# An mLSTM recurrence moved one chunk further ahead of the FFN that consumes it

## The chip, the cores and the metric

The kernel runs on one core of one Trainium2 chip. The metric is the device time of one execution in microseconds; the time of a kernel is the median of its runs. A profile is one further execution, recorded instruction by instruction.

TensorE multiplies matrices and accumulates in PSUM. VectorE and ScalarE work on tiles in SBUF and PSUM, GpSimd on tiles in SBUF. SyncE only issues DMAs, one after the other in the order of the program: where one waits, all behind it wait too. In profile rows the engines are PE (matmul), PEld (weight load), DVE (VectorE), ACT (ScalarE), POOL (GpSimd) and SPq (SyncE's queue).

## What is computed

An mLSTM cell (4 batches, 8 heads, 768 steps, head dimension 40) whose output, as 3072 tokens of 320 numbers, goes through a feed-forward network with squared ReLU. The reference, cut:

```python
for t in range(S):
    m_new = np.maximum(f_gate[:, :, t] + m, i_gate[:, :, t])
    f_stab = np.exp(f_gate[:, :, t] + m - m_new)
    i_stab = np.exp(i_gate[:, :, t] - m_new)
    m = m_new
    C = f_stab[:, :, None, None] * C + i_stab[:, :, None, None] * np.einsum('bhd,bhe->bhde', vt, kt)
    n = f_stab[:, :, None] * n + i_stab[:, :, None] * kt
    h_tilde = np.einsum('bhde,bhe->bhd', C, qt)
    nq = np.einsum('bhd,bhd->bh', n, qt)[:, :, None]
    denom = np.maximum(np.abs(nq), 1.0)
    o = 1.0 / (1.0 + np.exp(-o_gate[:, :, t]))
    y[:, :, t] = o * h_tilde / denom
# x: y as (3072, 320); w_in is 320 x 2048, w_out 2048 x 320
h = np.maximum(x @ w_in, 0.0)
out = h * h @ w_out
```

## The kernel before

**Tiling.** The sequence is cut into chunks of 128 steps: 6 chunks in each of 4 batches, 24 chunks in all, numbered 0 to 23. Within a chunk the recurrence is done as attention: scores k·q (`scores`, L423), times a matrix W of decays (`weighted`, L436, into the tiles `P_sb`), times v, plus the state C carried from the chunk before. At the first chunk of a batch there is no old state, at the last no new one. Two chunks form a group of the FFN, 12 groups. FFN1 (x by w_in, L644 and L655) has four parts per group, FFN2 (squares by w_out) four as well; from group 1 on FFN2 is done with seven half-size products instead of eight (`ffn2_fast`, L738), for which VectorE makes sums and differences of the squares (`sums`, L733).

**The path of a chunk's x in the second stage** (chunks 6 to 23), where transposes are made by VectorE in 32x32 squares and by DMAs that move the squares. `attend_turned` (L522, L511, L533) leaves numerators in PSUM; VectorE transposes them into `tn` (L544, one buffer); `store_num` (L556) writes them to DRAM, `load_num` (L561, four DMAs) reads them back in other order; `normalise_turned` (L573 to L582) divides and multiplies by the output gate into x; `store_rows` (L608) and `load_rows` (L613, four DMAs) take x through DRAM; `turn_squares` (L620) transposes the squares in place, and only then can FFN1 read x. Keys and queries take a like path: `pair_up` (L287, four DMAs within DRAM), `load_squares` (L309, four), `turn_kq` (L316). The decays come from `load_A` (L334, one DMA of 512 KB), exponentials on ScalarE (`decays` L369, `weigh` L383) and a mask on GpSimd (L359).

**The order** is written out by hand; every engine runs its instructions in the order in which the code issues them. A first stage (the loop over `u`, lines 873 to 930) does chunks 2 to 5 with FFN1 of groups 0 and 1, while the weights are fetched and rounded. The second stage is the loop over `parts` (line 977): entries (1, g, i) are parts of FFN1 of group g, (2, g, i) of FFN2. Entries 0 to 7 are FFN1 of group 2 and FFN2 of group 0. From entry 8 on a period has eight entries, `r` = 0 to 7: two parts of FFN2 of group g (r = 0, 1), four of FFN1 of group g+2 (r = 2 to 5), the other two of FFN2 (r = 6, 7). The parts of FFN1 go in pairs: two times L644, two times L655, and then `tiled()`, here called the tiled section: one chunk is attended and the scores of the next are made. So a period has two tiled sections, in r = 3 and r = 5. In the kernel before they attend chunks `a` = 6 + 2(n // 8) and a+1, while FFN1 reads chunks a−2 and a−1.

Buffers that matter: two `P_sb` tiles, so the tiles of the next chunk are those of the one before; four banks for scores and numerators; two `A_bc`, two `kqT`, two `xT` (one per group).

## Time and profile before

| | |
|---|---|
| runs | 7: 557.88 to 561.87 us, median 559.99 |
| profiled execution | 562.97 us, span of the profile 561.2 us |
| mean granted TensorE clock | 0.973 |
| busy share of the span | PE 94%, VectorE 59%, ScalarE 34%, GpSimd 16% |
| DMA | 68.06 MB, 56.5% of 16 engines' span in SyncE's queue |

A timeline row gives the start in us from the span's start, the time to the end of the last of its instructions, engine, line, operation, tiles, shape and count; in brackets the idle time ahead of the first one, and what ended it. A row of a window gives the window, its length, each engine's busy time with the number of instructions, and then TensorE's granted clock, the DMA share and GB/s. A row of DMAs gives how many, KB each, and the median time from issue to landing in us. One matmul of the program is recorded as two.

### The profile page before, as it was taken

To read this page: it belongs to the slowest core of one execution; us is meant where nothing else is said; L and a number is where in the kernel's file an instruction comes from. 1 tells how busy PE (TensorE), PEld (TensorE's weight loads), DVE (VectorE), ACT (ScalarE), POOL (GpSimd) and SP (SyncE) were. 2 spreads that over 40 slices of the span, in tenths; PEclk is the share of its full clock that TensorE was granted. 3 is DMA by queue.
4 is the path that set the end of the run, shared out by engine and by line. 5 is a ranking of instruction groups with operands and counts; after the bars stand their busy time and mean duration, and the time that the engine had idled before them with its cause. 6 is when DMAs were issued, how large, how long until landed. Compare 5 with 4: busy or idle time off the path is not lost.

```text
span 561.2 us, 10358 instructions
## 1 busy us (share of the span) xinstructions
PE 525.7 (94%) x3932; PEld 454.9 (81%) x3933; DVE 333.6 (59%) x638; ACT 192.6 (34%) x460; POOL 88.4 (16%) x110
## 2 busy tenths in 40 slices
PE   9998999999999699969979969988997999999997
PEld 4877887876988588958968958887896898898997
DVE  8579988678745437536645553753763764561351
ACT  3766587442361215304114331321532312101100
POOL 3336633132020001001001000110200100000000
PEclk9998999999999989979989998998999999999999
DMA  9979899766646827645764572782774460220000
GB/s 196 226 163 202 161 206 220 168 141 152 118 100 151 166 25 179 131 86 109 161 122 84 140 152 40 172 168 42 179 146 72 119 122 10 76 71 1 25 23 25
DMA packets 239394, 68.06 MB, mean 121 GB/s; under 512 B 185744, under 2 KB 233872, under 8 KB 239344
## 3 DMA queue, kind: packets, MB, share of 16 engines
q1 hardware_dynamic: 239248, 67.20, 56.5%
q8 instruction: 31, 0.51, 0.4%
q10 hardware_dynamic: 96, 0.20, 0.1%
q14 instruction: 19, 0.16, 0.1%
HBM read 55.08 MB, written 17.86 MB: 130 GB/s over the span
## 4 chain that ended last, share of the span: by engine, by line
PE 49%; DMA 22%; SPq 15%; DVE 8%; issue 3%; ACT 2%; POOL 0%; DVEq 0%; POOLq 0%
PE h_ps L644 25%; DMA x_rows<-x_sb 8%; PE h_ps L738 8%; PE h_ps L655 6%; SPq L613 5%; DMA xT<-x_rows 4%; DMA kq<-num_rows 3%; SPq L561 3%; DMA num_rows<-tn 3%; SPq L287 2%; DMA A_bc<-a_rows 2%; SPq L309 2%; PE tp L423 2%; PE numT L533 1%; PE idle L797 1%
## 5 line engine op out<-in xcount | busy, mean ns | idle before, releaser
L644 PE MATMUL h_ps<-xT,w_in 128*128 128x256 f32 x768 | 185.5, 402 | 27.9 <-DVE xT L620 18.1
L644 PEld LDWEIGHTS h_ps<-xT,w_in 128*128 128x128 f32 x768 | 152.3, 202 | 54.7 <-DVE xT L620 29.4
L670 ACT ACTIVATE r_sb<-h_ps 128x512 f32<-128x512 f32 x96 | 49.8, 599 | 163.1 <-issue 95.1
L677 DVE TENSOR_TENSOR g<-r_sb 128x512 f32<-128x512 f32 x96 | 69.7, 774 | 11.6 <-ACT r_sb L670 11.6
L738 PE MATMUL h_ps<-w_out,g 128*128 128x160 f32 x528 | 75.7, 299 | 0.0
L738 PEld LDWEIGHTS h_ps<-w_out,g 128*128 128x128 f32 x528 | 72.9, 190 | 0.4 <-DVE y_sb L754 0.2
L544 DVE STREAM_TRANSPOSE tn<-numT 128x256 f32<-128x256 f32 x36 | 15.8, 447 | 85.1 <-PE numT L533 84.6
L383 ACT ACTIVATE W_sb<-A_bc,b_T 128x128 f32<-128x128 f32 x176 | 53.8, 388 | 30.6 <-POOL A_bc L359 30.4
L738 PE MATMUL h_ps<-T,S 128*128 128x160 f32 x352 | 52.3, 302 | 0.0
L738 PEld LDWEIGHTS h_ps<-T,S 128*128 128x128 f32 x352 | 48.7, 190 | 1.4 <-ACT r_sb L670 0.3
L655 PE MATMUL h_ps<-xT,w_in 64*128 64x256 f32 x384 | 49.0, 391 | 0.0
L655 PEld LDWEIGHTS h_ps<-xT,w_in 64*128 64x128 f32 x384 | 34.8, 186 | 12.3 <-issue 9.3
L359 POOL TENSOR_SCALAR_AFFINE_SELECT A_bc<-A_bc 128x1024 f32<-128x1024 f32 x22 | 25.4, 1156 | 107.5 <-ACT kq L369 107.5
L754 DVE TENSOR_TENSOR y_sb<-y_sb,h_ps 128x160 f32<-128x160 f32 x44 | 13.7, 312 | 37.5 <-PE h_ps L738 37.5
L758 ACT COPY y_sb<-h_ps 128x160 f32<-128x160 f32 x11 | 3.2, 292 | 93.6 <-PE h_ps L738 93.6
L436 DVE TENSOR_TENSOR P_sb<-tp,W_sb 128x512 f32<-128x512 f32 x46 | 29.6, 686 | 8.3 <-PE tp L423 6.1
L620 DVE STREAM_TRANSPOSE xT<-xT 128x384 f32<-128x384 f32 x18 | 10.3, 573 | 40.6 <-DMA xT<-x_rows 40.6
L489 POOL TENSOR_TENSOR Cd<-C,kq 128x164 f32<-128x164 f32 x15 | 7.0, 464 | 165.3 <-DVE C L550 131.9
L423 PE MATMUL tp<-kqT 40*128 40x128 f32 x384 | 27.7, 284 | 1.1 <-ACT xT L629 1.1
L423 PEld LDWEIGHTS tp<-kqT 40*128 40x128 f32 x384 | 23.5, 187 | 5.2 <-issue 3.2
L395 POOL TENSOR_TENSOR vw<-va,W_sb 128x328 f32<-128x328 f32 x20 | 17.4, 872 | 54.0 <-ACT W_sb L383 37.0
L738 PE MATMUL h_ps<-w_out,S 128*128 128x160 f32 x176 | 25.7, 299 | 0.0
(119 smaller groups left out, 613.2 us busy)
## 6 DMA issues: line engine op xcount, KB each, us to landing
A_bc<-a_rows SPq DMA_DIRECT2D x23, 512.0 KB, 5.2
raw<-in_moe_w_out_dram SPq DMA_DIRECT2D x16, 320.0 KB, 3.5
num_rows<-tn SPq DMA_DIRECT2D x18, 256.0 KB, 2.4
kq<-num_rows SPq DMA_DIRECT2D x72, 64.0 KB, 2.1
kqT<-kq_rows SPq DMA_DIRECT2D x34, 128.0 KB, 3.2
raw<-in_moe_w_in_dram SPq DMA_DIRECT2D x8, 512.0 KB, 4.3
kq<-in_k_dram SPq DMA_DIRECT2D x24, 160.0 KB, 3.7
va<-in_v_dram SPq DMA_DIRECT2D x24, 160.0 KB, 4.1
```

The lines of the kernel that those rows point to most:

```text
L359: nc.gpsimd.affine_select(A[:], A[:], compare_op=ALU.is_ge, fill=-1e30, base=0, pattern=[[0, H], [1, P]], channel_multiplier=-1,)
L383: nc.scalar.activation(d["W"][:, i * n + h, :], A[i][:, h, :], AF.Exp, bias=b_T[:, b, c, i * n + h : i * n + h + 1],)
L395: nc.gpsimd.tensor_tensor(d["vw"][:], d["va"][:], d["W"][:, :, P - 1 : P].to_broadcast([P, H, D1]), op=ALU.mult,)
L423: nc.tensor.matmul(sc[i][:, j, :], lhsT=d["kT"][rows, j, :], rhs=d["qT"][rows, j, :], start=True, stop=True,)
L436: nc.vector.tensor_tensor(t, d["sc"][i], d["W"][:, heads, :], op=ALU.mult)
L561: nc.sync.dma_start(N[m * SQ : (m + 1) * SQ].rearrange("p (e c) -> p e c", c=P), n_d[s, :, m * P : (m + 1) * P].rearrange("(e p) c -> p e ...
L613: nc.sync.dma_start(t[r * SQ : (r + 1) * SQ].rearrange("p (b a) -> p b a", a=SQ), x_d[s, :, :, r * SQ : (r + 1) * SQ].rearrange("c (n p) a ...
L644: nc.tensor.matmul(hs[i][:, n, :], lhsT=w_in[:, a, fb * P : (fb + 1) * P], rhs=xT[:, :, a, :], start=(n == 0 and a == 0), stop=False,)
L655: nc.tensor.matmul(hs[i][:, n, :], lhsT=w_in2[rows, 2 * pp + n, :], rhs=xT[rows, :, 2, :], start=False, stop=(n == 1),)
L670: nc.scalar.activation(rs[-1][:], h[:], AF.Relu)
L677: nc.vector.tensor_tensor(g4[:, :, i, :], r[:], r[:], op=ALU.mult)
L738: nc.tensor.matmul(to, lhsT=lhsT[:, p], rhs=rhs[:, p, :], start=(start and p == 0), stop=(p == NPAIR - 1), skip_group_check=True,)
```

## The change

Nothing is computed in another way; the order of the work is another one.

- Second stage: the two tiled sections of a period now attend chunks `b` = 7 + 2(n // 8) and b+1, that is one chunk further on; FFN1 reads chunks b−3 and b−2. To get there, chunk 8 is attended in entry 9 (the tenth), inside FFN2 of group 1, with what it needs made earlier: its successor's squares, A and masks in entries 5 to 8. The last period with recurrence attends one chunk less.
- In a tiled section `score(x + 1)` comes ahead of `attend_turned(x)`.
- `turn_squares` of a period's second x moves from r = 1 to the end of r = 2, the loads of o from r = 3 to r = 5, the sigmoids from r = 5 to r = 3.
- First stage: `normalise` is split; its first sum (`sum_of_h`) frees a bank ahead of the rounding of a weight piece, and the first squares move behind a normalisation (from u = 0 to the end of u = 1). `turn_rows(5)` moves between L644 and L655 of the last part.
- The PSUM pool `ps_o` is opened first, so the later pool for scores begins with its banks.

```diff
+    ps_o = banks.enter_context(tc.tile_pool(name="ps_o", bufs=2, space=PSUM))
     ps_at = banks.enter_context(tc.tile_pool(name="ps_at", bufs=3, space=PSUM))
     ps_h = banks.enter_context(tc.tile_pool(name="ps_h", bufs=3, space=PSUM))
-    ps_o = banks.enter_context(tc.tile_pool(name="ps_o", bufs=2, space=PSUM))
...
-    def normalise(s):
+    def sum_of_h(s):
         d = st[s]
         num = d["num"]
         if num is not d["hp"]:
             nc.vector.tensor_tensor(num[:], num[:], d["hp"][:], op=ALU.add)
+
+    def normalise(s):
+        d = st[s]
+        num = d["num"]
         dm = work.tile([P, H], F32, name="dm")
...
                 weigh(s + 1)
-                square_half()
+                if u > 0:
+                    square_half()
...
             attend(s)
-            if u in (1, 3):
-                if u == 3:
-                    square_half()
+            if u == 3:
+                square_half()
+            sum_of_h(s)
+            if u == 3:
                 normalise(s)
-                rounding.join()
-            else:
-                rounding.join()
+            rounding.join()
+            if u != 3:
                 normalise(s)
...
             rounding.words()
-            ffn1(u // 4, u % 4)
-            square_half()
+            if u == 7:
+                ffn1_main(1, 3)
+                turn_rows(5)
+                ffn1_rest(1, 3, st["half"][0])
+                square_half()
+                relu_half()
+            else:
+                ffn1(u // 4, u % 4)
+                if u > 1:
+                    square_half()
...
+        if u == 1:
+            square_half()
-    relu_half()
     square_half()
-    turn_rows(5)
...
-    def attended(s):
+    def attended(s, early=False):
         do(store_num, s)
         do(load, s + 4)
         do(load_num, s)
+        if early:
+            load_squares(s + 2)
+            load_A(s + 2)
         do(pair_up, s + 3)
...
-        r, a = (n % 8, 6 + 2 * (n // 8)) if n >= 8 else (None, None)
+        r, b = (n % 8, 7 + 2 * (n // 8)) if n >= 8 else (None, None)
...
-            load_squares(a + 2)
-            load_A(a + 2)
+            load_squares(10)
+            load_A(10)
             sums_of_weights(3)
             sums(1, ALL, (3,))
+        if n == 9:
+            score(9)
+            attend_turned(8)
+            decay_C(9)
+            attended(8)
+            turn_squares(7)
+        if n == 12:
+            turn_squares(8)
 
         if r == 0 and g > 1:
-            do(turn_squares, a - 2)
+            do(turn_squares, b - 2)
             sums(g, ALL, (3,))
-        elif r == 1:
-            do(turn_squares, a - 1)
...
                 def tiled():
+                    do(score, x + 1)
                     do(attend_turned, x)
-                    do(score, x + 1)
...
+            decays(9)
+            mask(9)
+            turn_kq(9)
+        if n == 8:
+            masked_W(9)
+        elif n == 9:
+            load_A(11)
+            load_o(12)
+            load_o(13)
+            decays(10)
+            mask(10)
+        elif n == 10:
+            normalise_turned(8)
+            store_rows(8)
...
         elif r == 2:
-            do(masked_W, a + 1)
-            if a > 8:
-                do(load_squares, a + 2)
+            do(masked_W, b + 1)
+            do(load_squares, b + 2)
+            if g > 3:
+                do(turn_squares, b - 1)
+            if n == 10:
+                load_rows(8)
         elif r == 3:
-            do(decays, a + 2)
-            do(mask, a + 2)
-            attended(a)
-            for t in range(a + 4, min(a + 6, NT)):
-                load_o(t)
+            do(decays, b + 2)
+            do(mask, b + 2)
+            attended(b)
+            if b % 4 == 3:
+                for t in range(b + 1, min(b + 5, NT)):
+                    sigmoid(t)
...
         elif r == 5:
-            if (a + 1) % 4 == 3:
-                for t in range(a + 2, min(a + 6, NT)):
-                    sigmoid(t)
-            do(store_num, a + 1)
-            do(load_rows, a)
-            do(load_num, a + 1)
-            do(load, a + 5)
+            do(store_num, b + 1)
+            do(load_rows, b)
+            do(load_num, b + 1)
+            do(load, b + 5)
+            for t in range(b + 5, min(b + 7, NT)):
+                load_o(t)
```

The order in which the instructions stand, at the three places of which the prediction speaks. In the changed kernel lines behind `normalise` are four higher (L738 is L742, L620 is L624, and so on). TensorE from FFN2 of group 1 on, entries 8 to 11; `tp` is scores, `numT` the matmuls of a chunk (the `kq` and `va` it reads tell which: 87 and 91 are those of chunk 8). Before:

```order
L423 MATMUL tp<-kqT_95 128x128 x8
L738 MATMUL h_ps<-w_out,g_837 128x160 x8
L738 MATMUL h_ps<-T_1511,S_1514 128x160 x8
L738 MATMUL h_ps<-w_out,g_837 128x160 x16
L644 MATMUL h_ps<-xT,w_in 128x256 x16
L655 MATMUL h_ps<-xT,w_in_103 128x256 x8
L522 MATMUL numT<-kq_89,C_1188 64x128 x8
L511 MATMUL numT<-vw,kq_87 40x41 x8
L533 MATMUL numT<-P_sb,va_91 64x128 x8
L423 MATMUL tp<-kqT_96 128x128 x8
```

and in the changed kernel:

```order
L742 MATMUL h_ps<-T_1517,S_1520 128x160 x8
L423 MATMUL tp<-kqT_96 128x128 x8
L522 MATMUL numT<-kq_89,C_1188 64x128 x8
L511 MATMUL numT<-vw,kq_87 40x41 x8
L533 MATMUL numT<-P_sb,va_91 64x128 x8
L742 MATMUL h_ps<-w_out,g_837 128x160 x16
L648 MATMUL h_ps<-xT,w_in 128x256 x16
L659 MATMUL h_ps<-xT,w_in_103 128x256 x8
L423 MATMUL tp<-kqT_95 128x128 x8
L522 MATMUL numT<-kq_90,C_1187 64x128 x8
L511 MATMUL numT<-vw,kq_88 40x41 x8
L533 MATMUL numT<-P_sb,va_92 64x128 x8
```

Chunk 8 and the scores of chunk 9 now stand within FFN2, ahead of FFN1 of group 3, and in each section the scores stand first. VectorE from r = 1 over the first tiled section of a period in the steady part (`y_sb` are additions of FFN2, `g` squares, `S` the sums of `sums`). Before:

```order
L620 STREAM_TRANSPOSE xT<-xT 128x384
L754 TENSOR_TENSOR y_sb<-y_sb,h_ps 128x160
L677 TENSOR_TENSOR g_1995<-r_sb 128x2x256 x2
L733 TENSOR_TENSOR S_1515<-g_1645,S_1514 128x1024
L316 STREAM_TRANSPOSE kqT_96<-kqT_96 128x1024
L544 STREAM_TRANSPOSE tn<-numT 128x2x4x32 x2
L552 COPY C_1187<-numT 40x164 x2
L436 TENSOR_TENSOR P_sb<-tp,W_sb 128x512 x2
```

and in the changed kernel:

```order
L758 TENSOR_TENSOR y_sb<-y_sb,h_ps 128x160
L681 TENSOR_TENSOR g_2090<-r_sb 128x2x256 x2
L737 TENSOR_TENSOR S_1521<-g_1726,S_1520 128x1024
L484 TENSOR_TENSOR kq_90<-kq_90,kqT_96 128x512
L316 STREAM_TRANSPOSE kqT_95<-kqT_95 128x1024
L624 STREAM_TRANSPOSE xT<-xT 128x384
L436 TENSOR_TENSOR P_sb<-tp,W_sb 128x512 x2
L544 STREAM_TRANSPOSE tn<-numT 128x2x4x32 x2
L550 TENSOR_TENSOR C_1188<-numT,Cd 40x164 x2
```

The turn of x has moved behind the additions, sums and the turn of the keys, and the multiplies into `P_sb` ahead of the transposes into `tn`. SyncE's queue from the stores of x in r = 5 (`store_rows`) to the store of a finished row in r = 6. Before, with the loads of o ahead of it:

```order
L324 DMA og<-in_o_gate_dram 128x8x40 x2
L334 DMA A_bc<-a_rows 128x8x128
L608 DMA x_rows<-x_sb 128x3x128
L556 DMA num_rows<-tn 128x512
L613 DMA xT<-x_rows 32x12x32 x4
L561 DMA kq_88<-num_rows 32x4x128 x4
L296 DMA kq_88<-in_k_dram 128x8x40
L296 DMA va_92<-in_v_dram 128x8x40
L774 DMA out_dram<-y_sb 128x320
```

and in the changed kernel:

```order
L334 DMA A_bc<-a_rows 128x8x128
L612 DMA x_rows<-x_sb 128x3x128
L556 DMA num_rows<-tn 128x512
L617 DMA xT<-x_rows 32x12x32 x4
L561 DMA kq_87<-num_rows 32x4x128 x4
L296 DMA kq_89<-in_k_dram 128x8x40
L296 DMA va_93<-in_v_dram 128x8x40
L324 DMA og<-in_o_gate_dram 128x8x40 x2
L778 DMA out_dram<-y_sb 128x320
```

The loads of o have moved behind the loads of the numerators; the rest stands as before.

More of the change, by code (lines that the diff above doesn't have):

```diff
@@ L853 @@
     rounding.step()
+    sum_of_h(0)
     normalise(0)
@@ L856 @@
     attend(1)
+    sum_of_h(1)
     normalise(1)
@@ L998 @@
                 turn_squares(s - 1)
-            attended(s)
+            attended(s, early=(n == 5))
         if n == 6:
@@ L1061 @@
             store_rows(s)
-            load_squares(s + 2)
+            if n == 2:
+                load_squares(s + 2)
             load_rows(s)
-            load_A(s + 2)
+            if n == 2:
+                load_A(s + 2)
         if n == 7:
@@ L1067 @@
                 sigmoid(t)
-        if r == 0:
-            do(decays, a + 1)
-            do(mask, a + 1)
+            decays(9)
[12 more added lines that the diff above has]
+            store_rows(8)
+        if r == 0 and g > 1:
+            do(decays, b + 1)
+            do(mask, b + 1)
             square_half()
@@ L1073 @@
             if g > 1:
-                do(pair_up, a + 2)
+                do(pair_up, b + 2)
             square_half()
@@ L1077 @@
                 sums(g, ALL, (4,))
[L1078 to L1080 removed]
+            do(scale_q, b)
+            do(turn_kq, b + 1)
         elif r == 2:
[L1082 to L1090 removed]
+            do(masked_W, b + 1)
[4 more added lines that the diff above has]
+                load_rows(8)
+        elif r == 3:
+            do(decays, b + 2)
[4 more added lines that the diff above has]
+                    sigmoid(t)
         elif r == 4:
@@ L1093 @@
             square_half()
-            do(masked_W, a + 2)
-            do(load_A, a + 3)
+            do(masked_W, b + 2)
+            do(load_A, b + 3)
         elif r == 5:
-            if (a + 1) % 4 == 3:
-                for t in range(a + 2, min(a + 6, NT)):
-                    sigmoid(t)
-            do(store_num, a + 1)
-            do(load_rows, a)
-            do(load_num, a + 1)
-            do(load, a + 5)
+            do(store_num, b + 1)
[4 more added lines that the diff above has]
+                load_o(t)
         elif r == 6:
-            do(load_squares, a + 3)
+            do(load_squares, b + 3)
         elif r == 7:
-            do(load_A, a + 4)
-            do(load_rows, a + 1)
+            do(load_A, b + 4)
+            do(load_rows, b + 1)
         if which == 2 and g == NG - 1 and i == 0:
```

17 lines of the change are left out of this document (7 added, 10 removed).

## The prediction

> **What bounds the kernel now.** I read the busy table first, then TensorE's waits, the timeline at each place where it stood still, the clock around those places, and at last one period of the steady part on all engines. The busy row, and the waits by what ended them (us in total, times, longest):
>
> ```profile
> PE 525.7 (94%) x3932; PEld 454.9 (81%) x3933; DVE 333.6 (59%) x638; ACT 192.6 (34%) x460; POOL 88.4 (16%) x110
> ```
>
> ```profile
> PE h_ps L644 <- DVE xT L620: 18.1, 7, 5.2
> PE h_ps L644 <- DMA kq_rows<-in_q_dram: 9.1, 2, 5.6
> PE tp L411 <- DVE num L465: 1.9, 1, 1.9
> PE tp L423 <- ACT xT L629: 1.1, 1, 1.1
> ```
>
> TensorE is busy for 94% of the span, and nearly all that it waits for is one thing: L644, the first matmul of an FFN1 batch, waits for the turned squares of x. The second row gives another releaser by the profile, but it is the same instruction at the same place of the loop. The nine batches of groups 3 to 11 in the timeline, each with the wait ahead of it:
>
> ```profile
> 150.91 7.17 PE L644 MATMUL h_ps<-xT,w_in 128*128 128x256 f32 x32 [0.39 <-DVE xT L620]
> ...
> 196.08 9.51 PE L644 MATMUL h_ps<-xT,w_in 128*128 128x256 f32 x32 [5.59 <-DMA kq_rows<-in_q_dram]
> ...
> 242.83 10.03 PE L644 MATMUL h_ps<-xT,w_in 128*128 128x256 f32 x32 [5.13 <-DVE xT L620]
> ...
> 288.14 8.86 PE L644 MATMUL h_ps<-xT,w_in 128*128 128x256 f32 x32 [3.48 <-DMA kq_rows<-in_q_dram]
> ...
> 334.66 10.19 PE L644 MATMUL h_ps<-xT,w_in 128*128 128x256 f32 x32 [5.24 <-DVE xT L620]
> ...
> 380.34 8.86 PE L644 MATMUL h_ps<-xT,w_in 128*128 128x256 f32 x32 [3.38 <-DVE xT L620]
> ...
> 424.29 7.17 PE L644 MATMUL h_ps<-xT,w_in 128*128 128x256 f32 x32 [3.28 <-DVE xT L620]
> ...
> 464.29 7.17 PE L644 MATMUL h_ps<-xT,w_in 128*128 128x256 f32 x32 [0.42 <-DVE xT L620]
> ...
> 502.76 7.17 PE L644 MATMUL h_ps<-xT,w_in 128*128 128x256 f32 x32 [0.28 <-DVE xT L620]
> ```
>
> The same 32 matmuls take 7.17 us in four batches and 8.86 to 10.19 in the five behind waits of 3.38 us and more. The granted clock says why:
>
> ```profile
> 196.10:203.30 7.20, 7.20 (x23) 5.93 (x24) 4.23 (x6) 0.00 (x0) 0.00 (x0) 0.67 0.43 54
> ...
> 424.30:431.40 7.10, 7.10 (x33) 5.99 (x34) 4.24 (x6) 0.00 (x0) 0.00 (x0) 1.00 0.45 57
> 424.29:464.29 40.00, 39.59 (x336) 35.27 (x336) 24.54 (x50) 11.66 (x30) 3.97 (x5) 1.00 0.44 96
> ```
>
> The third column from the right is the clock: 0.67 behind the wait of 5.59 us, 1.00 behind that of 3.28. So each long wait is paid twice.
>
> **Why x is late.** One period of the steady part, from the tiled section of part r=3 (TensorE at 298.86, called T) on. DVE, SP and TensorE rows:
>
> ```profile
> 291.29 2.37 SPq L309 DMA_DIRECT2D kqT<-kq_rows  x4
> ...
> 298.86 0.67 PE L522 MATMUL numT<-kq,C 40*64 40x128 f32 x16
> ...
> 300.47 0.89 DVE L544 STREAM_TRANSPOSE tn<-numT 128x256 f32<-128x256 f32 x2 [8.08 <-PE numT L533]
> ...
> 300.79 1.16 PE L423 MATMUL tp<-kqT 40*128 40x128 f32 x16
> ...
> 301.38 0.34 SPq L556 DMA_DIRECT2D num_rows<-tn  x1
> ...
> 302.05 1.29 DVE L436 TENSOR_TENSOR P_sb<-tp,W_sb 128x512 f32<-128x512 f32 x2
> ...
> 304.02 1.23 DVE L316 STREAM_TRANSPOSE kqT<-kqT 128x1024 f32<-128x1024 f32 x1
> ...
> 308.10 0.16 DVE L573 TENSOR_SCALAR dm<-kq 128x8 f32<-128x8 f32 x1
> ...
> 308.61 1.21 SPq L324 DMA_DIRECT2D og<-in_o_gate_dram  x2
> ...
> 310.80 0.58 SPq L608 DMA_DIRECT2D x_rows<-x_sb  x1
> ...
> 310.91 0.67 PE L522 MATMUL numT<-kq,C 40*64 40x128 f32 x16
> ...
> 313.52 1.55 ACT L327 ACTIVATE og<-og 128x320 f32<-128x320 f32 x4
> ...
> 315.86 1.86 SPq L613 DMA_DIRECT2D xT<-x_rows  x4
> ...
> 317.82 1.84 SPq L561 DMA_DIRECT2D kq<-num_rows  x4
> ...
> 322.36 0.17 DVE L573 TENSOR_SCALAR dm<-kq 128x8 f32<-128x8 f32 x1 [2.32 <-DMA kq<-num_rows]
> ...
> 324.31 0.57 DVE L620 STREAM_TRANSPOSE xT<-xT 128x384 f32<-128x384 f32 x1
> ...
> 324.80 1.18 DVE L733 TENSOR_TENSOR g<-g 128x1024 f32<-128x1024 f32 x1
> 324.90 4.51 PE L738 MATMUL h_ps<-w_out,g 128*128 128x160 f32 x32
> ...
> 334.02 0.58 DVE L620 STREAM_TRANSPOSE xT<-xT 128x384 f32<-128x384 f32 x1 [5.91 <-DMA xT<-x_rows]
> ```
>
> The second chunk of a group is attended in part r=5 (310.91). Its numerators go out and come back through DRAM and are normalised from 322.36, 23.5 us after T; then x goes out and back too (L608, L613) and VectorE turns it at 334.02. Between the two lie only the four FFN2 parts, 313.9 (310.91 and a section of 3.0) to 329.4, so TensorE is out of work 5.2 us early. A period without its wait and slow clock is short: 242.83 − 196.08 = 46.75 us, less the wait of 5.13 at its end and the 2.34 of slow clock at its start, gives 39.28; the 40.00 of the row from 424.29, less 0.42, gives 39.58 with all its VectorE work.
>
> **The change, part by part.**
>
> *One chunk further ahead.* An FFN1 batch still needs both chunks of its group, but the later one is now attended in r=3 of the period before (not r=5) and the other one a whole period earlier. The later one's x would be turned where the first chunk's is now, in r=0, some 4 us before r=2 begins (the turn at 324.31, which waits for nothing; r=2 could begin at 334.66 − 5.24 = 329.4). So the waits of the eight batches from 196.08 on go: 5.59 + 5.13 + 3.48 + 5.24 + 3.38 + 3.28 + 0.42 + 0.28 = 26.8 us. With them goes the slow clock, each batch's excess over 7.17: 2.34 + 2.86 + 1.69 + 3.02 + 1.69 = 11.6 us. What hides the way through DRAM is now two more FFN1 parts and a tiled section; if that cover were gone, the 38.4 us would be back.
>
> On the clock the Trainium skill, "TensorE: Matmul & The Clock Gate", section "A second HAM failure mode: psum-queue depth-cycling", has a rule against this: short idle moments between matmul groups, frequent enough, make the clock swing as long ones do. By that rule the 11.6 us would stay. The row from 424.29 (0.42 us of waits, clock 1.00) disagrees.
>
> *Chunk 8's tiled section moved up to the tenth part (n=9), and the first period behind it.* One tiled section, 298.86 to the end of the scores at 301.95, some 3.0 us, comes earlier and falls away in the last period with recurrence: nothing in TensorE's sum. load_squares(9) and load_A(9) go ahead of pair_up(10) and of store_rows(7): five issues, 2.37 + about 0.5 us, by which x(7) is later at worst; FFN1 of group 3 reads it 2.6 later anyway. But the first period has to catch up. SP is in order, and load_rows(8) now stands ahead of store_num(9). I follow it with the medians from issue to landing:
>
> ```profile
> A_bc<-a_rows SPq DMA_DIRECT2D x23, 512.0 KB, 5.2
> ...
> num_rows<-tn SPq DMA_DIRECT2D x18, 256.0 KB, 2.4
> kq<-num_rows SPq DMA_DIRECT2D x72, 64.0 KB, 2.1
> ...
> x_rows<-x_sb SPq DMA_DIRECT2D x18, 192.0 KB, 2.8
> ```
>
> FFN1 of group 3 would start at 153.5 (150.91, less 0.39, plus 3.0), so the next tiled section is at 162.5 (9.0 on, two main batches and their rest) and tn(9) is ready 4.9 us later (below), at 167.4. Chunk 8's section begins one FFN2 part (4.5, the 324.90 row) ahead of 150.5, at 146.0: matmuls 3.0, two multiplies 1.3, tn 0.9, so tn(8) at about 151.5. From there: store_num 0.4 + 2.4, load_num 1.8 + 2.1, normalise 1.8 (from 322.36; the turn at 324.31 stands behind it and one add), store 0.1 + 2.8, load_rows 1.9: 164.8, in time. If both stores run behind an A load, as the one at 310.80 does (landed by 315.86, 5.06 us instead of 2.8), it is 169.8, 2.4 us late. That lateness passes down SP to the next normalisation and the FFN2 part behind it: a wait of at most 2.4 us, or with a slow clock behind it (1.69 to 3.02) up to 5.4. Bounds 0 and 5.4; I take 2, between, because an A load does stand ahead of each of the two.
>
> *Scores first in the tiled section.* TensorE does the same matmuls in another order. VectorE's multiplies (1.29 us) now stand ahead of the transposes of tn, and they need the P buffers that chunk x's matmuls still read; behind them are tn, the sums into C, scale_q and turn_kq. Before, tn was done at 301.36 = T+2.5. Now: 16 score matmuls first (1.1 us), then numT's first half, so the multiplies run from T+2.6 to T+3.9 and tn from there to T+4.8: 2.3 us later. TensorE does not wait for it. SP does: store, load_num and the normalisation in r=5 come 2 us later (308.10 becomes about 310.1, after the squares), the x store 1.1 later (310.80 was held by load_o until 309.82 and an A load, and load_o has moved behind load_num). What hangs on it is the r=7 normalisation and then L733 on g, whose output the second product of the 324.90 row reads (it starts half-way, at 327.1; L733 ends at 325.98: 1.1 us of slack). The nearest row, 310.80 to 315.86, has og and A ahead of it; without og I expect the landing at about the same time as now. So: 0 per period at best, 2.3 − 1.1 = 1.2 at worst, I say 1.5 since the slack won't be the same in each; I take 0.2 in seven periods, 1.5 us in all.
>
> *First squares behind a normalisation, sums of h first, joins after them.* VectorE's order ahead of 53 us. The wait of L411 for L465 (1.9 us) loses the squares ahead of it, but these parts also wait for rounded weights, which come no sooner, so I take 0; bounds −1.9 (all of it gained) and 0.
>
> *One x turn inside an FFN part, other banks first.* turn_rows(5) comes between L644 and L655 and the first scores of the steady part use banks that were long free: the 1.1 us of L423 go.
>
> *turn_squares and sigmoid moved.* VectorE's turn of the second x stands behind turn_kq, so it blocks nothing TensorE waits for; ScalarE's four sigmoids (313.52) now stand ahead of the W exponentials of r=4, which a section reads later; ScalarE is busy for 11.66 of 40.00 us there. I take 0 for both; were W late, it is the 1.55 us of the sigmoids in every second period.
>
> Sum: 561.2 − 26.8 − 11.6 − 1.1 + 2 + 1.5 = 525.2 us of span. The median of the runs, 559.99, lies 1.2 below that span (the profiled execution, 562.97, lies 1.8 above it), so I forecast 525.2 − 1.2 = **524.0**.
>
> **Rivals.**
> 1. *The FFN2 product becomes the new wait.* If the 2.3 us do reach L733 in full, TensorE waits 1.2 to 1.5 us in each of eight periods, and the start its 5.4: 524 − 1.5 + 8 × 1.35 + 3.4 = 536.7. For it: L573 in r=7 already waits 2.32 us for its load. Against it: that load hangs on the x store, not on tn. Chance 0.15.
> 2. *The start costs a full wait with a slow clock, the rest is as forecast:* 524 + 3.4 = 527.4. Chance 0.07.
> 3. *The clock swings on short waits* (the rule named above): 524 + 11.6 = 535.6. Chance 0.03, since 0.42 us of waits left the clock at 1.00.
> 4. *Slower.* Scores first means TensorE can't attend before the next chunk's turned keys are there. The place is turn_kq in r=4: it ends at 305.25, 5.7 us before the section at 310.91, and runs 2.3 us later now: 3.4 us of slack. If SP fell behind with the squares (291.29), TensorE would stand in both sections. It decides when they are over 5.8 us later than now (2.4 us lost in each of 15 sections eats the 36); at 3 us each it is 524 + 45 = 569. Against it: SP is idle from 293.66 to 301.38, 7.7 us. Chance 0.04.
> 5. *The gain is not there* because x is late for another reason in the in-order queue: 557 to 561. Chance 0.03.
>
> **How the numbers follow.** The forecast has 0.68 with its own range of 518.6 (both costs 0, the 1.9 gained) to 530. The range down to 518 and up to 538 takes in rivals 1 to 3 and leaves out 4 and 5 and some of the rest. Faster by over 0.3% (1.7 us, about what these runs can tell from no change): the forecast and rivals 1 to 3, 0.93; of rival 5 0.02 are the same and 0.01 slower, with rival 4 0.05 slower.
>
> **What would show it.** Right: no wait over 1 us ahead of L644 from group 4 on, the 32 matmuls at 7.17 us in each batch, clock 1.00 from some 200 us to the end, periods of 39.3 to 39.6 us. The start's term: a wait in the FFN2 parts between 180 and 195 us of up to 2.5. Scores first: tn at T+4.8, L733 on g still ahead of the product that reads it. Wrong: waits of over 1 us at L738 or L423 in every period (rivals 1 and 4), or a clock under 1.00 without a wait over 3.3 us (rival 3).

## The result and the profile after

The changed kernel takes 531.61 us (median of 12 runs, 527.30 to 533.25) against 559.99 of the kernel before (31 runs): a ratio of 0.9488, 95% interval 0.9465 to 0.9512. Its profiled execution took 531.65 us with a span of 529.9 and a mean granted clock of 0.990. The forecast was 524.0, so the gain is 28.4 us where 36.0 were foretold. Direction and mechanism were right; 7.6 us are missing.

Of the changed kernel, first the busy row, then TensorE's waits (us in total, times, longest):

```profile
PE 512.3 (97%) x3932; PEld 450.5 (85%) x3933; DVE 333.8 (63%) x638; ACT 193.7 (37%) x460; POOL 91.0 (17%) x110
```

```profile
PE h_ps L742 <- DVE y_sb L758: 8.1, 4, 3.7
PE h_ps L648 <- POOL w_in L215: 3.0, 2, 1.8
...
PE h_ps L648 <- DVE xT L624: 0.2, 1, 0.2
```

The 27.2 us in which FFN1 waited for x are 0.2 now. In their place stand two waits that were not there: 8.1 us ahead of FFN2 products (L742, the former L738) and 3.0 us for rounded weights (`w_in`) in the first stage. The FFN1 batches of groups 4, 5 and 7 in the timeline:

```profile
197.52 7.61 PE L648 MATMUL h_ps<-xT,w_in 128*128 128x256 f32 x32
...
236.70 7.07 PE L648 MATMUL h_ps<-xT,w_in 128*128 128x256 f32 x32
...
316.18 7.07 PE L648 MATMUL h_ps<-xT,w_in 128*128 128x256 f32 x32
```

No bracket, so no wait, and 7.07 to 7.61 us instead of 9.51 to 10.19. Where the time went is seen by cutting both kernels at the same points of the program: the begin of FFN1 of groups 2, 3, 4, 10 and 11. Before (window, length, busy time of each engine with its instructions, clock, DMA share, GB/s):

```profile
99.45:150.91 51.46, 50.70 (x339) 40.54 (x337) 38.26 (x72) 18.73 (x46) 11.50 (x13) 1.00 0.68 143
150.91:196.08 45.17, 39.58 (x336) 35.27 (x337) 23.29 (x47) 17.14 (x42) 5.75 (x7) 0.98 0.67 142
196.08:464.29 268.21, 247.29 (x1952) 218.53 (x1952) 147.59 (x289) 81.45 (x194) 25.85 (x32) 0.95 0.57 118
464.29:502.76 38.47, 38.19 (x304) 34.00 (x304) 21.07 (x45) 4.92 (x11) 0.47 (x1) 1.00 0.22 57
```

and in the changed kernel:

```profile
98.22:152.19 53.97, 53.64 (x400) 43.09 (x400) 44.06 (x81) 25.89 (x62) 15.51 (x19) 1.00 0.74 157
152.19:197.52 45.33, 40.78 (x336) 36.72 (x337) 25.49 (x54) 14.78 (x38) 5.81 (x7) 0.97 0.76 161
197.52:436.66 239.14, 234.73 (x1953) 213.43 (x1953) 149.19 (x288) 79.59 (x186) 26.12 (x30) 0.99 0.62 128
436.66:471.56 34.90, 34.90 (x242) 31.41 (x241) 15.04 (x29) 4.71 (x10) 0.00 (x0) 1.00 0.13 37
```

The column that matters is the length. Against it the forecast, stretch by stretch from its own terms:

| stretch | before | forecast | after |
|---|---|---|---|
| start to FFN1 of group 2 | 99.45 | 98.35 (−1.1) | 98.22 |
| to group 3 (a tiled section more) | 51.46 | 54.5 (+3.0) | 53.97 |
| to group 4 (the start of the new order) | 45.17 | 41.6 (−5.59 + 2) | 45.33 |
| to group 10 (six steady periods) | 268.21 | 236.9 (waits −20.9, clock −11.6, +1.2) | 239.14 |
| to group 11 (a tiled section less) | 38.47 | 35.4 (−3.0 − 0.28 + 0.2) | 34.90 |
| to the end | 58.44 | 58.44 | 58.34 |
| span | 561.2 | 525.2 | 529.9 |

So 3.7 us are missing in one period, the first, and 2.2 in the six behind it. The rest of the 7.6 is no work of any engine: the profiled execution of before lay 3.0 us above its median, and I carried that over; that of the changed kernel lies on its median.

**What is late there.** VectorE, ScalarE, SyncE and TensorE of the changed kernel at the end of the first period:

```profile
187.45 2.77 SPq L324 DMA_DIRECT2D og<-in_o_gate_dram  x2
187.93 0.17 DVE L573 TENSOR_SCALAR dm<-kq 128x8 f32<-128x8 f32 x1 [3.60 <-DMA kq<-num_rows]
...
190.32 0.57 SPq L778 DMA_DIRECT2D out_dram<-y_sb  x1
190.37 1.18 DVE L737 TENSOR_TENSOR g<-g 128x1024 f32<-128x1024 f32 x1
...
193.71 0.29 ACT L767 COPY y_sb<-h_ps 128x160 f32<-128x160 f32 x1 [7.31 <-DMA out_dram<-y_sb]
193.73 0.33 DVE L758 TENSOR_TENSOR y_sb<-h_ps,y_sb 128x160 f32<-128x160 f32 x1 [2.18 <-DMA out_dram<-y_sb]
...
194.11 3.62 PE L742 MATMUL h_ps<-w_out,g 128*128 128x160 f32 x16 [3.69 <-DVE y_sb L758]
```

and four periods later:

```profile
354.47 0.29 ACT L767 COPY y_sb<-h_ps 128x160 f32<-128x160 f32 x1 [5.14 <-DMA out_dram<-y_sb]
354.49 0.33 DVE L758 TENSOR_TENSOR y_sb<-h_ps,y_sb 128x160 f32<-128x160 f32 x1 [0.97 <-DMA out_dram<-y_sb]
...
354.87 3.94 PE L742 MATMUL h_ps<-w_out,g 128*128 128x160 f32 x16 [2.69 <-DVE y_sb L758]
```

TensorE waits for an addition into `y_sb` that empties its bank. The addition comes late for two reasons, one on top of the other. The normalisation of r = 7 (L573) waited 3.60 us for its numerators and stands ahead of L737 and of the addition on VectorE; L737 is done at 191.55. Then the addition itself waits 2.18 us more, until an output row has been stored: there are three row buffers, and it writes into the one that held a row of the FFN2 parts just done. The store (L778) was issued at 190.32, behind the two loads of o (187.45 + 2.77 = 190.22), which the change has put there. The product that follows takes 3.62 and 3.94 us instead of 2.44, at half clock. My reading of these rows, then: the change moved the loads of o off the path of x onto that of the output rows. The rival: the normalisation alone (the prediction's rival 1), and the order of the tiled section behind it.

### The profile page after: what moved, and what is told of

The parts are those of the page before. It is cut to its first block, busy times and chain, and to the rows that moved or that the text cites. A ratio compares the mean times of both kernels' runs of the same rounds, so it can differ in the third digit from the quotient of the medians.

```text
span 529.9 us, 10358 instructions
## 1 busy us (share of the span) xinstructions
PE 512.3 (97%) x3932; PEld 450.5 (85%) x3933; DVE 333.8 (63%) x638; ACT 193.7 (37%) x460; POOL 91.0 (17%) x110
## 4 chain that ended last, share of the span: by engine, by line
PE 67%; DMA 14%; SPq 9%; DVE 6%; issue 2%; ACT 1%; POOL 1%; DVEq 0%; POOLq 0%; ACTq 0%
PE h_ps L648 24%; PE h_ps L742 19%; PE h_ps L659 6%; DMA x_rows<-x_sb 3%; DMA kq<-num_rows 3%; DMA out_dram<-y_sb 3%; PE tp L423 3%; SPq L617 3%; PE h_ps L688 3%; SPq L561 2%; PE hp L459 2%; PE numT L533 2%; DMA num_rows<-tn 2%; SPq L324 2%; PE idle L801 1%
## 5 line engine op out<-in xcount | busy, mean ns | idle before, releaser
L648 PE MATMUL h_ps<-xT,w_in 128*128 128x256 f32 x768 | 174.7, 385 | 4.1 <-POOL w_in L215 3.0
L648 PEld LDWEIGHTS h_ps<-xT,w_in 128*128 128x128 f32 x768 | 145.8, 193 | 26.4 <-POOL w_in L215 3.6
L742 PE MATMUL h_ps<-w_out,g 128*128 128x160 f32 x528 | 79.3, 307 | 8.1 <-DVE y_sb L758 8.1
L742 PEld LDWEIGHTS h_ps<-w_out,g 128*128 128x128 f32 x528 | 75.3, 195 | 9.4 <-DVE y_sb L758 9.1
L681 DVE TENSOR_TENSOR g<-r_sb 128x512 f32<-128x512 f32 x96 | 68.1, 759 | 10.0 <-ACT r_sb L674 10.0
L383 ACT ACTIVATE W_sb<-A_bc,b_T 128x128 f32<-128x128 f32 x176 | 53.8, 388 | 26.8 <-POOL A_bc L359 26.6
L742 PE MATMUL h_ps<-T,S 128*128 128x160 f32 x352 | 52.3, 302 | 0.0
L742 PEld LDWEIGHTS h_ps<-T,S 128*128 128x128 f32 x352 | 48.8, 190 | 1.6 <-ACT r_sb L674 0.8
L359 POOL TENSOR_SCALAR_AFFINE_SELECT A_bc<-A_bc 128x1024 f32<-128x1024 f32 x22 | 28.2, 1281 | 70.1 <-ACT kq L369 57.2
L423 PEld LDWEIGHTS tp<-kqT 40*128 40x128 f32 x384 | 24.8, 188 | 3.6 <-PE h_ps L659 1.2
L423 PE MATMUL tp<-kqT 40*128 40x128 f32 x384 | 26.3, 276 | 0.9 <-PE h_ps L659 0.9
L369 ACT ACTIVATE kq<-A_bc 64x512 f32<-64x512 f32 x30 | 18.9, 629 | 19.8 <-DMA A_bc<-a_rows 17.9
L742 PE MATMUL h_ps<-T,g 128*128 128x160 f32 x176 | 25.7, 299 | 0.0
L742 PE MATMUL h_ps<-w_out,S 128*128 128x160 f32 x176 | 25.7, 299 | 0.0
```

Source lines behind the costliest of these rows:

```text
L359: nc.gpsimd.affine_select(A[:], A[:], compare_op=ALU.is_ge, fill=-1e30, base=0, pattern=[[0, H], [1, P]], channel_multiplier=-1,)
L369: nc.scalar.activation(e[rows], st[s]["A"][0][rows, PR * i : PR * (i + 1), :], AF.Exp)
L383: nc.scalar.activation(d["W"][:, i * n + h, :], A[i][:, h, :], AF.Exp, bias=b_T[:, b, c, i * n + h : i * n + h + 1],)
L423: nc.tensor.matmul(sc[i][:, j, :], lhsT=d["kT"][rows, j, :], rhs=d["qT"][rows, j, :], start=True, stop=True,)
L648: nc.tensor.matmul(hs[i][:, n, :], lhsT=w_in[:, a, fb * P : (fb + 1) * P], rhs=xT[:, :, a, :], start=(n == 0 and a == 0), stop=False,)
L681: nc.vector.tensor_tensor(g4[:, :, i, :], r[:], r[:], op=ALU.mult)
```

## The experiments

### Taking away the two suspects behind the FFN2 wait

Two kernels against the row store: a fourth buffer for it, or the loads of o behind it. First the fourth buffer:

```diff
-            st["y"] = [ffn.tile([P, DM], F32, name="y_sb", bufs=3) for _ in range(2)]
+            y1 = ffn.tile([P, DM], F32, name="y_sb", bufs=3)
+            y0 = attn.tile([P, DM], F32, name="y_odd", bufs=1) if g % 2 else ffn.tile([P, DM], F32, name="y_sb", bufs=3)
+            st["y"] = [y1, y0]
```

> The changed kernel with a fourth buffer for finished rows (y0 of odd groups has one of its own), nothing else. Theory Y (the FFN2 waits of 8.1 us come from the three row buffers: the add into y0 waits until the row stored before has landed): the waits at L742 fall from 8.1 to about 2.8 us, what the turned squares of g then still hold up in two periods, and the two slow-clock stretches (3.4 us) go: 531.6 - 8.7 = 523. Theory N (rival 1 as the prediction had it: the numerators come back late, so the difference of squares on g is late): the waits stay, 531 to 532.

Measured: 527.31 us, ratio to before 0.9391 (0.9344 to 0.9439), span 523.6, so between the two expectations. The waits at L742 fall from 8.1 to 3.1 us, in two places (1.75 at 194.85, 1.34 at 350.32), neither of them behind a store.

The loads of o one entry later, behind the issue of the row store:

```diff
             do(load, b + 5)
-            for t in range(b + 5, min(b + 7, NT)):
-                load_o(t)
         elif r == 6:
             do(load_squares, b + 3)
+            for t in range(b + 5, min(b + 7, NT)):
+                load_o(t)
```

> The changed kernel with the two loads of o moved from the end of r=5 to the end of r=6, behind the store of the finished row on SyncE's queue. Theory Y: that store goes out 2.8 us earlier (190.3 becomes 187.5), lands ahead of the add that waits for it, and the time is that of the fourth buffer, 523 to 525. If the store is late for what stands ahead of the loads of o (the loads of the numerators), at most a third of it: 529. Theory N: 531 to 532.

Measured: 525.52 us, ratio 0.9370 (0.9321 to 0.9419), span 523.1, half a microsecond above the 523 to 525 of the first theory. The same place of the program as above, in this kernel:

```profile
189.18 1.50 SPq L778 DMA_DIRECT2D out_dram<-y_sb  x1
189.58 0.17 DVE L573 TENSOR_SCALAR dm<-kq 128x8 f32<-128x8 f32 x1 [3.42 <-DMA kq<-num_rows]
...
193.16 0.33 DVE L758 TENSOR_TENSOR y_sb<-h_ps,y_sb 128x160 f32<-128x160 f32 x1
...
193.43 1.50 SPq L324 DMA_DIRECT2D og<-in_o_gate_dram  x2
193.54 2.44 PE L742 MATMUL h_ps<-w_out,g 128*128 128x160 f32 x16 [1.36 <-DVE y_sb L758]
```

The addition has no wait of its own any more, and the product takes 2.44 us. What stays, 1.36 us, belongs to the normalisation, which still waits for its numerators. So both layers are real: the row store cost some 2.2 us and the slow clock behind it, the normalisation some 1.4.

Was it the chip? Both kernels once more, side by side on one chip:

> The changed kernel as it is, on the chip of the three beside it. Both theories: 531.6 us as before, between 529 and 534, with waits at L742 of some 8 us in all and slow clock behind those over 2.6 us.

> The loads of o behind the row store (r=5 to r=6), once more. If the row store behind the loads of o is what costs the changed kernel its last microseconds: 525 to 527 us, that is 4 to 7 below the changed kernel on the same chip, and no slow clock behind 60 us. If the difference seen so far was one of chips: within 2 us of the changed kernel.

The changed kernel 529.69 us (ratio 0.9462, 0.9419 to 0.9505), with the loads of o behind 526.75 (0.9396, 0.9354 to 0.9438). Side by side the intervals still overlap a little; over all runs the medians are 531.5 (18 runs) against 525.7 (12 runs). So the loads of o behind the store are the better kernel, by some 3 to 6 us. Two expectations fell. The second profile with the loads behind has half clock at 178 us, behind an L423 wait of 1.89 us (see the last section). And in the changed kernel's second profile the waits at L742 are 4.7 us, not some 8, with no half clock behind them: single executions differ by some 2 to 3 us in these places.

Both edits together:

> The loads of o behind the row store and a fourth row buffer. If the row buffers set what is left of the waits in the steady part (0.52 and 1.32 us at L742 with the loads of o moved), these two go and the one at the start, which a normalisation sets, stays: span 521 to 522, time 523 to 525. If they are set by something else, the same as with the loads of o moved alone, 525.5.

525.09 us (0.9390, 0.9345 to 0.9434), span 522.7, waits at L742 of 1.97 at the start and 0.52 at 233.58. By its time it can't be told from the loads of o alone. The wait near 350 us is gone, but its row in the kernel beside it (1.64 us) was behind the normalisation and not a store, so that is no proof for the buffer.

### The order within a tiled section

The changed kernel with the old order, attend first:

```diff
                 def tiled():
-                    do(score, x + 1)
                     do(attend_turned, x)
+                    do(score, x + 1)
```

> The changed kernel with the sections in the order of before: chunk x attended, then the scores of x+1. The prediction's term (2.3 us on tn, 0.2 us a period on TensorE): 530 to 531.6. Theory Y: tn is 2.3 us earlier, so the loads of the numerators and, behind them in the queue, the store of the finished row go out up to 1 us earlier: 527 to 530. If scores first were worth something for TensorE itself: 533 or more.

529.97 us, ratio 0.9433 (0.9386 to 0.9481), span 529.4: where two of the three expectations meet, so the time does not choose between them. No wait at L742 in any period behind the first, but a longer one in it:

```profile
193.46 0.17 DVE L573 TENSOR_SCALAR dm<-kq 128x8 f32<-128x8 f32 x1 [6.62 <-DMA kq<-num_rows]
...
198.41 3.83 PE L742 MATMUL h_ps<-w_out,g 128*128 128x160 f32 x16 [5.06 <-DVE y_sb L758]
```

So scores first does cost the steady periods some waits (numerators 2.2 us later, the row store behind them), and it gives about as much back at the start. The same with the loads of o behind:

> The loads of o behind the row store, and a tiled section attends first, as in the kernel before. If the order of the section costs the steady part only through the row buffer, nothing is left there to gain: no wait at L742 behind 210 us, and the start as long as with attending first in the changed kernel (two waits of some 6 us in all, one of them long enough for a slow clock): 527 to 530. If scores first costs each period by itself, it is faster than with the loads of o moved alone: 523 or less.

529.17 us (0.9428, 0.9382 to 0.9473); the waits are 1.14 at 183.44 and 3.74 at 196.14, then none. By its numbers the first of the two expectations came true, but it doesn't show that the order costs only through the row buffer. With the loads of o behind and scores first, the steady part kept two waits at L742, 0.52 and 1.32 us, in which the addition did not wait for a store; with attend first they are gone too. So late numerators cost the steady part some 2 us by themselves, and the start, which is longer with attend first, takes back more than that.

Scores first alone, in the kernel before, is another matter:

```diff
                 def tiled():
-                    do(attend_turned, x)
                     do(score, x + 1)
+                    do(attend_turned, x)
```

> The kernel before with only the sections turned round: scores of x+1 first, then chunk x. There the way of x through DRAM is the bound, so the 2.3 us by which tn is later would show in full if they reached it: up to 8 x 2.3 = 18 us slower, 578, and slow clocks with it. By the prediction's reading (what hangs on it is the x store's chain, 1.1 us later at the store and 0 at its landing): 560 to 565.

578.34 us, ratio 1.0357 (1.0302 to 1.0412), span 573.5, clock 0.955. TensorE's waits, and one section (scores at 299.73, called T):

```profile
PE h_ps L644 <- DMA kq_rows<-in_q_dram: 12.6, 4, 4.4
PE h_ps L644 <- DVE xT L620: 12.5, 5, 4.8
PE h_ps L738 <- DVE y_sb L754: 10.7, 5, 3.5
```

```profile
299.73 1.06 PE L423 MATMUL tp<-kqT 40*128 40x128 f32 x16
...
302.40 1.29 DVE L436 TENSOR_TENSOR P_sb<-tp,W_sb 128x512 f32<-128x512 f32 x2 [10.37 <-PE numT L533]
...
303.61 0.77 DVE L544 STREAM_TRANSPOSE tn<-numT 128x256 f32<-128x256 f32 x2
...
304.41 0.34 SPq L556 DMA_DIRECT2D num_rows<-tn  x1
```

The numerators are stored at T + 4.7 instead of T + 2.5, and those 2.2 us reach TensorE: 35.8 us of waits in place of 27.2, now in two places of a period, and behind the first 60 us half clock for 44 us instead of 27. By the ratio the move costs 20 us. The wait ahead of the FFN2 product here stands behind the normalisation. It is the prediction's rival 1 at full price, in the old kernel, where the way of x is the bound. The same move costs the changed kernel nothing that its time shows.

### One part alone, and one part undone

The part "one chunk further ahead" alone: the changed kernel with its first stage as before and with attend first. The small moves of the second stage (`turn_squares`, the loads of o, the sigmoids) stay in it.

> The recurrence one chunk further ahead and nothing else of the change's order: first stage as in the kernel before, sections attend first and score second. The forecast's terms: 26.8 + 11.6 us less, 2 for the start: 523 to 527. By the runs so far (attend first 530.0, first stage as before 530.8, neither told from the change's 531.6): 529 to 531, and nearly the whole of the gain is this one part.

529.38 us, ratio 0.9470 (0.9416 to 0.9524), span 528.8: as good as the whole change. All of the gain is this part with its small moves; what those are worth without it, no run shows.

The first stage alone undone (`normalise` in one piece, the first squares at u = 0, `turn_rows(5)` behind the loop, `ps_o` opened last):

```diff
-                ffn1_main(1, 3)
-                turn_rows(5)
-                ffn1_rest(1, 3, st["half"][0])
...
+            ffn1(u // 4, u % 4)
+            square_half()
...
+    turn_rows(5)
```

> The changed kernel with the first stage of the kernel before (normalisation in one piece, squares and turn_rows(5) where they were, ps_o opened last). The prediction had 1.1 us for turn_rows and 0 (bound 1.9) for the rest: 532.7, bound 534.6. FFN1 of group 2 starts at 98.2 in the changed kernel and 99.5 before, so 532.9 by the profile.

530.84 us (0.9451, 0.9404 to 0.9498), not the 532.7 expected, and not to be told from the changed kernel. The waits of L411 (1.9) and L423 (1.06) are back and the two of 1.25 and 1.77 for rounded weights are gone. FFN1 of group 2 begins at 99.44 in this execution and at 99.1 to 100.3 in the others with the old first stage; with the changed one it begins at 98.22 in the first profile and at 98.9 to 100.6 in eight others. So the edits of the first stage trade one wait for another.

### What the slow clock costs by itself

The kernel before, with some 3.2 us of zero matmuls ahead of FFN1's first product in six periods, so that TensorE is busy while it waits for x (`idle(0)` issues no matmul, it only takes a PSUM buffer):

```diff
         if which == 1:
+            if 16 <= n < 60 and i == 0:
+                idle(14)
+                for _ in range(3):
+                    idle(0)
             ffn1_main(g, i)
```

> The kernel before, with 14 matmuls of zeros (3.1 us) ahead of FFN1's first in the six periods whose wait is 3.28 to 5.59 us. They add work that nothing reads. If the slow clock behind a wait costs the 11.6 us that the prediction took from the batches' excess: the clock stays at 1.00 there, each batch takes 7.17 us, 548. If the excess is part of the same wait (x late, the loop as long as before): 560, the time only moves from the batch into the wait.

549.56 us, ratio 0.9862 (0.9812 to 0.9912), span 547.7, clock 0.993. One of the six places, and the whole stretch of the six (clock in the third column from the right):

```profile
234.75 3.23 PE L797 MATMUL idle<-zeros 128*128 128x512 bf16 x14
...
239.78 7.17 PE L644 MATMUL h_ps<-xT,w_in 128*128 128x256 f32 x32 [1.81 <-DVE xT L620]
```

```profile
190.00:460.00 270.00, 264.04 (x2093) 227.01 (x2091) 153.25 (x295) 84.02 (x202) 26.56 (x32) 1.00 0.58 121
```

x is as late as ever (3.23 + 1.81 us, with 5.13 before), but the batch takes 7.17 us instead of 10.03. By the ratio the clock's share is 7.7 us (4.9 to 10.5). By the two spans it is 13.5, but the profiled execution of before was 3 us long, so some 10.5. My term of 11.6 is a little high for both. The price of the clock is one of its own, apart from the wait.

### The turn of x(8) and the wait at L423

In the first period VectorE stands for x(8) and turns the next keys behind it, and the scores wait (0.51 to 2.25 us at L423 in different executions). With the loads of o behind, the turn was moved two entries later:

```diff
-        if n == 12:
-            turn_squares(8)
...
         elif r == 6:
+            if n == 14:
+                turn_squares(8)
```

> The changed kernel with the loads of o behind the row store (as in e2_o_behind) and the turn of chunk 8's x moved from the start of n=12 to the end of n=14, where VectorE no longer waits for it ahead of the turn of chunk 11's keys. In e2_o_behind VectorE stood 5.7 us at that turn and TensorE 1.3 us at the scores of chunk 11: they go, 1.3 us less than e2_o_behind, 524.2. If the keys themselves are late, no change.

530.32 us (0.9477, 0.9423 to 0.9531; 5 runs), span 523.6. The wait at L423 is gone, and the next one grew:

```profile
190.55 0.17 DVE L573 TENSOR_SCALAR dm<-kq 128x8 f32<-128x8 f32 x1 [5.29 <-DMA kq<-num_rows]
...
194.46 2.44 PE L742 MATMUL h_ps<-w_out,g 128*128 128x160 f32 x16 [3.55 <-DVE y_sb L758]
```

TensorE arrives earlier at the FFN2 product and waits there for the same numerators, which come no earlier (L573 at 190.55, against 189.58 with the loads of o behind alone). So the numerators set the start, and the turn of x(8) only decided at which of two instructions TensorE stands. The 524.2 that I expected lies below all five runs (525.34 was the lowest), and by the ratios this kernel is no faster than the loads of o behind alone (0.9370 and 0.9396), more likely slower.

## Why the prediction was right and wrong

*The wait for x (26.8 us): right.* 0.2 us of it are left, and the chunk-ahead part with its small moves has the whole gain.

*The slow clock behind it (11.6 us): right as a price of its own, in size a little high.* The five batches went back to 7.07 to 7.61 us, and the zero matmuls show the price without the change (7.7 us, 4.9 to 10.5). But 3.4 us of half clock came back twice behind 60 us, after the new waits at L742.

*The tiled section moved (nothing in sum): right.* +2.5 us at one end, −3.6 at the other, the latter with the wait of 0.28.

*The start (2 us, bounds 0 to 5.4): wrong, and above its bounds.* The period came out 5.8 us above 45.17 − 5.59. The step that failed is my walk down SP's queue. It had tn(8) right (ready at 151.5; it is stored at 151.01), but its only worry was two A loads. It left out the two loads of o that the tenth entry issues ahead of the store of x(8), and the loads of squares that stand ahead of the loads of x(8):

```profile
160.54 2.55 SPq L324 DMA_DIRECT2D og<-in_o_gate_dram  x2
...
160.78 0.20 DVE L582 COPY x_sb<-x_sb 128x64 f32<-128x64 f32 x1
...
163.19 1.60 SPq L612 DMA_DIRECT2D x_rows<-x_sb  x1
164.89 2.71 SPq L309 DMA_DIRECT2D kqT<-kq_rows  x4
167.69 2.06 SPq L617 DMA_DIRECT2D xT<-x_rows  x4
...
169.86 0.42 SPq L556 DMA_DIRECT2D num_rows<-tn  x1
...
171.59 0.58 DVE L624 STREAM_TRANSPOSE xT<-xT 128x384 f32<-128x384 f32 x1 [5.27 <-DMA xT<-x_rows]
```

x(8) is ready at 160.98, but its store comes at 163.19, where my sum has it at 160.0. Its loads come at 167.69, behind 2.71 us of squares, and my sum had no time for their landing: x(8) can be turned at 171.59, not at 164.8 to 169.8. The lateness passes down the queue, as I had said, only more of it: the numerators of chunk 9 are stored at 169.86, behind the loads of x(8), where I had them ready at 167.4, and those of the chunk behind are normalised at 187.93. The rest is the place above: that normalisation, and the row store. I read this chain off the trace; no run moves the two loads of o or the squares of the tenth entry, so what they cost of the 5.8 us stays open.

*Scores first (0.2 us a period, 1.5 in all): the size was wrong, the reason too.* tn came where I had it (T + 4.7 for T + 4.8). My sum followed it to L733 on g and left 1.1 us of slack there. It named the right product as the one that would wait, but the addition into `y_sb`, which that product needs for its bank, was in no step: it stands behind the normalisation, behind L737 and, through the row buffer, behind a store. The steady periods of the first profile lost 0.35, 1.37 and 2.69 us to it and 1.6 to the clock, 6.0 us for my 1.5; in the second profile 2.7 of waits and no half clock. The table shows only 3.4 of these 6.0 (2.2 above a forecast that held 1.2): TensorE's busy time in the six periods came out some 2.6 us lower than before, the slow clock of both taken off, and why is open.

*"load_o has moved behind load_num", costed as a gain for x alone: the common cause.* I asked what the loads of o no longer delay, and not what stands behind their new place. It was the row store.

*Edits of the first stage (1.1 us): the waits went as said, the gain did not come.* I had allowed that the rounding of weights is the next bound for the squares, and not for `turn_rows(5)`; the run with the old first stage shows no difference in time.

*Relation of span and median (−1.2): 2.9 us of the miss.* The span of one execution was 3 us long; taking it as the base and the difference to the median as fixed mixed two executions.

*The rivals.* The first (a wait at the FFN2 product, 536.7) came true in part: in the place named, but by the normalisation and, on top of it, a store. Its argument against itself, that the load hangs on the x store and not on tn, fell: scores first alone cost the old kernel 20 us. Its full price needs the old kernel, where nothing hides the 2.2 us. The second came true by half: the start cost 5.8 us, a full wait with a slow clock behind it, where it had 5.4, but the rest was not as forecast. Of the third the sign that I had named appeared, half clock without a wait over 3.3 us (behind 2.69 us in the first profile, 1.97 in the second), but not its mechanism: waits of 0.35 and 1.37 us left the clock at 1.00, and it fell behind single windows in which TensorE did little (last section). The fourth (slower, keys late) did not happen: no section of the steady part waits for keys. Nor did the fifth: 0.2 us of the wait for x are left.

*The signs named.* No wait over 1 us was left ahead of FFN1 from group 4 on, and the batches took 7.07 to 7.61 us, as said. The clock did not stay at 1.00 (0.50 once in the steady part), and of the six steady periods four took 38.92 to 39.18 us but two 40.55 and 42.42, where 39.3 to 39.6 was foretold. At the start the wait was 3.69 us, not up to 2.5. Of the signs of being wrong, waits of over 1 us at the FFN2 product came in three of the periods, not in every one.

## What to carry to other kernels

When an issue is moved within an in-order queue, list what stands behind its new place as carefully as what stood behind the old one; here two loads that left the way of x delayed a store, and through three buffers an addition, a bank and a matmul. A move that costs 20 us where a path is the bound can cost nothing once that path has slack, so parts of a change are not to be priced in the old kernel one by one. And a stall has a second price, the slow clock behind it, which some useless matmuls can buy off when the stall itself can't be removed.

## What the runs showed of the hardware

The prediction took waits of 3.38 us and more to slow the clock and 3.28 not to. The runs show that the wait's length does not decide. The stretches of half clock in the trace of before begin at 194.019, 241.806 and 289.593 us, 14 times 3.413 us apart, and last 3.413 or 6.827 us; in every run they begin on such a grid, which lies differently against the start of the program in each (0.63 us in the changed kernel's first profile, 2.87 in that of before). What goes with them, behind 60 us, is how long TensorE was busy in the grid window ahead. Windows of before around its waits of 3.38 and 3.28 us:

```profile
374.92:378.34 3.42, 2.03 (x15) 1.79 (x14) 0.00 (x0) 2.63 (x9) 0.68 (x1) 1.00 0.83 190
378.34:381.75 3.41, 1.41 (x7) 1.26 (x8) 2.05 (x5) 0.00 (x0) 0.06 (x1) 1.00 0.44 106
381.75:385.17 3.42, 3.42 (x10) 2.67 (x9) 2.23 (x2) 0.00 (x0) 0.00 (x0) 0.50 0.76 82
...
419.30:422.71 3.41, 1.71 (x13) 1.47 (x11) 0.00 (x0) 2.34 (x8) 0.74 (x1) 1.00 0.93 204
422.71:426.13 3.42, 1.84 (x9) 1.64 (x10) 2.47 (x5) 0.00 (x0) 0.00 (x0) 1.00 0.31 86
426.13:429.50 3.37, 3.37 (x17) 2.98 (x16) 2.40 (x3) 0.00 (x0) 0.00 (x0) 1.00 0.32 42
```

The first wait left TensorE 1.41 us of work in one window (0.41), and the next ran at 0.50; the second was split over two (0.50 and 0.54), and nothing happened. So a wait of 1.97 us is enough when it falls into one window, as in the second profile of the changed kernel:

```profile
173.23:176.64 3.41, 1.44 (x15) 1.00 (x14) 2.80 (x4) 0.00 (x0) 0.00 (x0) 1.00 0.89 184
176.64:180.05 3.41, 3.41 (x51) 2.86 (x50) 2.01 (x5) 2.39 (x4) 0.00 (x0) 0.50 0.36 94
```

and the 3.55 us in the kernel with the late turn of x(8), split into windows with 0.47 and 0.49, left it at 1.00. In the 14 traces of the two kernels and the twelve runs, of the grid windows at full clock behind 60 us, all 27 in which TensorE was busy for 0.447 or less were followed by half clock (seven of them at the very end of a run), and none of those with 0.449 or more. Two things stay open. Ahead of 60 us half clock followed 15 windows of 0.30 to 1.00, seven of them at 46 to 48 us with 0.60 to 0.63, so the busy share can't be all that counts there. And how long half clock lasts, one to three windows, does not follow from it: the window at 176.64 above was busy throughout, and the next one still ran at 0.50.

The Trainium skill, "TensorE: Matmul & The Clock Gate", section "What's actually happening", says that the window is 3413 ns long and runs free of the kernel; the trace agrees with both. Its section "Why this matters for your kernels" advises to keep gaps under some 3 us; here 1.97 us was too long and 3.55 was not.
